# Turning the hidden rows of a 64-token expert slot: two row blocks stacked in one tile, four transposes a slot instead of eight

## The chip, the cores and the metric

The kernel runs on one core of a Trainium2 chip. The metric is the device time of one execution in microseconds (us), as a median of runs. The engines are TensorE (PE for its matmuls, PEld for its weight loads), VectorE (DVE), ScalarE (ACT), GpSimd (POOL) and SyncE (SP).

## The reference, cut

Attention over 24 heads feeds a dense two-layer block, and that feeds a mixture of eight experts in which each of the 896 tokens goes to one expert. The change lies in the last part:

```python
for e in range(E):                       # E = 8 experts, D = 768, F = 1024
    mask = expert_idx == e
    h = np.maximum(x[mask] @ w1[e], 0.0)
    out[mask] = gate_w[mask, None] * (h @ w2[e])
```

All inputs are float32. The kernel splits each operand into a high and a low part (`hi`, `lo`) and multiplies them in parts, so that one product of the reference is two or three matmul passes.

## The kernel before, in words

The expert part works on *slots*: a slot is up to so many tokens of one expert, which are gathered from `ydram`, multiplied by `w1` (`mm1`), passed through a ReLU, multiplied by `w2` (`mm2`), scaled by the gate and scattered to the output. An early slot and the remainder of the same expert (form M, 160 tokens) come first; then the slots run in the order T, M, T, L, T. Form L has up to 384 tokens, in two passes (D with 256, S with 128), form T has 64. So there are three T slots, called T1, T2 and T3 here; in the trace T1 lies at 413.4 to 427.4 us, T2 at 454.4 to 468.0, T3 at 520.2 to 532.8. Only they are changed; the S pass shares the function with them but keeps its own way.

In a T slot `mm1_x` takes the tokens as the stationary operand, high parts in columns 0 to 63, low parts in 64 to 127, and streams four blocks `q` of 256 weight columns. `two_pass` gives PSUM rows 0 to 63 (high) and 64 to 127 (low times high weights). For each `q` ScalarE copies the lower rows out (L1021) and VectorE adds the upper rows (L1022); the sum `hr` has 64 rows of tokens. Then the hidden units must be on partitions for `mm2`, so `turn` transposes `hr` on TensorE, two 128x128 transposes (L991) a block. Rows 64 to 127 of the tile are zeros that GpSimd wrote (L1015). ScalarE applies the ReLU for the high part (L994) and VectorE forms the low part (L995).

The order of the PE, ACT and DVE instructions in the slots is written out by hand: each engine runs them in program order. What is interleaved matters here:

- `turn(0)` and `turn(1)` stand before step `kc` 5 of `q` 2 and 3; `turn(2)` and `turn(3)` stand before steps `fc` 1 and 3 of `mm2` (`turn2=[1, 3]`).
- At the end of each `q`, behind the copy and the add, `pace` may put the split of one weight tile of the next slot into the queues: a 128x768 `mh` on ScalarE (L65) and an `ml` on VectorE (L72). The same is done after each `fc` of `mm2`. A T slot earns 0.5 of a split per `q` and 0.65 per `fc`.
- The evictions of the slot before (`osb`, L1069 to L1072) stand at the head of the ScalarE and VectorE queues when a T slot begins.
- The transposes of the next slot's tokens (`xt`, L1096) stand before `fc` 3 to 6 of `mm2`.

PSUM banks for `hps`, `ht` and `xt` come from `bank`, which goes round four of them.

Of the kernel before, what the change touches and what calls it, by code (L numbers as in the profile page):

```python
# [12 lines left out]
AF = mybir.ActivationFunctionType  # L13
ALU = mybir.AluOpType
# [6 lines left out]
P = 128  # L21
# [11 lines left out]
def f32(ap):  # L33
    return ap.bitcast(F32)


CFG = dict(
    first=1, hp=3000, xe=[1, 7, 8, 10, 12], turn=5, xfd=[3, 4, 5, 6], xfj=[1, 2, 3, 4],
    joint=1, mhi="A", rt6=[1, 4, 7, 9, 15], dve=(0, 1, 2, 3), neng=(),
    rs={2: [(1, 0), (2, 1)], 3: [(2, 2), (2, 0), (10, 1)], 4: [(1, 3), (5, 2)],  # L40
        5: [(2, 3), (2, 4), (3, 4), (4, 4), (5, 4), (7, 4)], 6: [(f, 5) for f in (1, 4, 7, 9, 15)]},
# [12 lines left out]
def build(tc, qkd, vd, w_in, w_out, emb, tau, wm, cst, out, dbg_y=None):  # L54
    nc = tc.nc
    V, A, G, T, DMA = nc.vector, nc.scalar, nc.gpsimd, nc.tensor, nc.sync
# [30 lines left out]
    ident = cpool.tile([P, P], F32, name="ident")  # L87
# [357 lines left out]
    for k in range(-3, 2 * NU + 2):  # L445
        u, h = divmod(k, 2)
# [376 lines left out]
    mo = {}  # L823
# [10 lines left out]
    def h_at(fs, part, n, m=1):  # L834

        hb = mo["h"][:, fs, part:part + m] if m > 1 else mo["h"][:, fs, part]
        return hb[..., 0:n], hb[..., n:2 * n]
# [3 lines left out]
    def bank(name):  # L841

        state["bank"] += 1
        if state["routed"] and state["bank"] % 4 == 0:
            return ps_r.tile([P, 512], F32, tag="lg", name=name)
        return ps_h.tile([P, 512], F32, tag="h", name=name)
# [47 lines left out]
    def pace(x, cap=2.7):  # L894

        if not fd["seq"]:
            return
        fd["credit"] = min(fd["credit"] + x, cap)
        while fd["credit"] >= 1 and fd["done"] < min(fd["free"], 16 * (len(fd["seq"]) - 1)):
            feed_one()  # L900
            fd["credit"] -= 1
# [22 lines left out]
    def mm1_w(s, w, hooks, fin=nop):  # L924
# [42 lines left out]
        fin(6)  # L967
        fin(7)

    def two_pass(os, x, whs, wls, k, n, m):  # L970

        def high():
            for o, w in zip(os, whs):
                T.matmul(o[0:2 * m], x, w, start=(k == 0), stop=(k == n - 1))  # L974

        if k == 0:
            high()
        for o, w in zip(os, wls):
            T.matmul(o[0:m], x[:, 0:m], w, start=False, stop=False)  # L979
        if k:  # L980
            high()

    def mm1_x(s, w, hooks, fin=nop):

        xh, xl = mo["xh"], mo["xl"]
        n = FORM[s[0]][0]

        def turn(q, hr):
            ht = bank("ht")[:, 0:2 * P].rearrange("p (a b) -> p a b", b=P)
            for j in range(2):  # L990
                T.transpose(ht[:, j], hr[:, j * P:(j + 1) * P], ident)  # L991
            ht = ht[:, :, 0:n]
            hi, lo = h_at(slice(2 * q, 2 * q + 2), 0, n)
            A.activation(hi, ht, AF.Relu)  # L994
            V.scalar_tensor_tensor(out=lo, in0=ht, scalar=0.0, in1=f32(hi), op0=ALU.max, op1=ALU.subtract)  # L995

        hrs = []
        for q in range(4):
            ps = bank("hps")[:, 0:256]
            for kc in range(KC):  # L1000
                step(hooks, (q, kc))
                if kc == CFG["turn"] and q >= 2:
                    turn(q - 2, hrs[q - 2])
                wh, wl = w[2 * q + kc // 3]
                c = slice((kc % 3) * 256, (kc % 3 + 1) * 256)
                if n == P:
                    T.matmul(ps, xh[:, kc, 0:P], wh[:, c], start=(kc == 0), stop=False)
                    T.matmul(ps, xh[:, kc, 0:P], wl[:, c], start=False, stop=False)
                    T.matmul(ps, xl[:, kc, 0:P], wh[:, c], start=False, stop=(kc == KC - 1))
                else:  # L1010
                    two_pass([ps], xh[:, kc, 0:P], [wh[:, c]], [wl[:, c]], kc, KC, n)
            if q % 2 == 0:
                hr2 = hpool.tile([P, 512], F32, tag="hs", bufs=4, name="hr")
                if n < P:
                    G.memset(hr2[n:P], 0.0)  # L1015
            hr_ = hr2[:, (q % 2) * 256:(q % 2 + 1) * 256]
            hr = hr_[0:n]
            if n == P:
                A.copy(hr, ps)
            else:  # L1020
                A.copy(hr, ps[64:P])  # L1021
                V.tensor_tensor(out=hr, in0=ps[0:64], in1=hr, op=ALU.add)  # L1022
            hrs.append(hr_)
            fin(2 * q)
            fin(2 * q + 1)
            pace(CFG["pc"][s[0]][0], CFG["cap"])

        rest = iter([lambda: turn(2, hrs[2]), lambda: turn(3, hrs[3])])
        return {t: [(f() for f in rest)] for t in CFG["turn2"]}

    def mm2(parts, w, hooks, split=False, fin=nop):

        at = (0, CFG["tail"] if split else 384, DM)
        col = [slice(at[c], at[c + 1]) for c in range(2)]
        pss = [[ps_y.tile([P, 512], F32, tag=f"y{c}", name="ops")[:, :at[c + 1] - at[c]] for c in range(2)]
               for _ in parts]
        for cs in ((0,), (1,)) if split else ((0, 1),):
            for fc in range(8):
                if cs[0] == 0:
                    step(hooks, fc)  # L1040
                wh, wl = w[8 + fc]
                for (s, part), ps in zip(parts, pss):
                    if FORM[s[0]][part] == P:
                        hh, hl = h_at(fc, part, P) if s[0] != "M" else (
                            mo["hm"][:, fc, 0:P], mo["hm"][:, fc, -P:])
                        for x, ww in ((hh, wh), (hh, wl), (hl, wh)):
                            for c in cs:
                                T.matmul(ps[c], x, ww[:, col[c]],  # L1048
                                         start=(fc == 0 and x is hh and ww is wh), stop=(fc == 7 and x is hl))
                    else:  # L1050
                        m = FORM[s[0]][part]
                        x = mo["hm"][:, fc, P:P + 2 * m] if s[0] == "M" else mo["h"][:, fc, part, 0:2 * m]
                        two_pass([ps[c] for c in cs], x,
                                 *([ww[:, col[c]] for c in cs] for ww in (wh, wl)), fc, 8, m)
                if cs[-1] == 1:
                    fin(8 + fc)
                    pace(CFG["pc"][parts[-1][0][0]][1])
        for (s, part), ps in zip(parts, pss):
            mm2_out(s, part, ps, col)

    def mm2_out(s, part, ps, cols):
        gi, si, gate = s[1][:3]
        col = s[2] + part
        n = FORM[s[0]][part]
        o = hpool.tile([P, DM], F32, tag="hs", bufs=4, name="osb")[0:n]
        for c in range(2):
            oc = o[:, cols[c]]
            if n == P:
                A.activation(oc, ps[c], AF.Copy, scale=gate[:, col:col + 1])  # L1069
            else:  # L1070
                A.activation(oc, ps[c][n:2 * n], AF.Copy, scale=s[1][3][n:2 * n, col:col + 1])
                V.scalar_tensor_tensor(out=oc, in0=ps[c][0:n], scalar=gate[0:n, col:col + 1], in1=oc,  # L1072
                                       op0=ALU.mult, op1=ALU.add)
        G.indirect_dma_start(out=out[:, :], out_offset=bass.IndirectOffsetOnAxis(ap=si[0:n, col:col + 1], axis=0),  # L1074
                             in_=o, in_offset=None, bounds_check=NT - 1, oob_is_err=False)
# [27 lines left out]
    def step(hooks, key):  # L1103
        for x in hooks.get(key, ()):
            next(x, None)
# [21 lines left out]
    def mm1(s, w, hooks, fin=nop):  # L1127
        return (mm1_w if s[0] in "DM" else mm1_x)(s, w, hooks, fin)
# [7 lines left out]
    for t in range(2, NTI):  # L1136
# [10 lines left out]
        if t == NTI - 1:  # L1147
# [6 lines left out]
            xe = slot_x(eslot)  # L1154
# [129 lines left out]
    def run_slot(ps, w, feeds, at_end=False):  # L1284

        def hooks_for(at, it, more=None):
            hooks = more or {}
            for k in at:
                hooks.setdefault(k, []).append(it)
            return hooks  # L1290

        s = ps[0]
        if len(ps) == 2:
            more = mm1(s, w, {})
            it = slot_x(ps[1])
            next(it)
            mm2([(s, 0)], w, hooks_for(CFG["xfd"], it, more))
            all_of(it)
            more = mm1(ps[1], w, {}, freed)
            it = feeds()  # L1300
            next(it, None)
            mm2([(s, 1), (ps[1], 0)], w, hooks_for(CFG["xfj"], it, more), fin=freed)
            all_of(it)
            return
        more = mm1(s, w, {}, freed)
        it = feeds()
        next(it, None)
        mm2([(s, i) for i in range(len(FORM[s[0]]))], w, hooks_for(CFG["xfd"], it, more), split=at_end, fin=freed)
        all_of(it)
# [140 lines left out]
```

## Time and profile before

| | |
|---|---|
| median of 3 runs | 542.87 us (542.78 to 543.02) |
| profiled execution | 543.2 us |
| its span, first to last instruction | 541.5 us |
| mean granted TensorE clock | 0.996 |
| PE busy | 527.2 us, 97% of the span |
| DVE, ACT, POOL busy | 413.5, 287.4, 205.6 us |

Times in the trace count from the start of the span. The profiled execution is 0.33 us above the median, and 1.7 us of it lie outside the span.

### The profile page before, as it was taken

The numbers are of one execution on the slowest core, as the hardware profiler recorded it, in microseconds if no ns is written. First come the engines' busy times: TensorE is split into PE (matmuls) and PEld (weight loads), VectorE is DVE, ScalarE is ACT, GpSimd is POOL, SyncE is SP. The second block draws the span as 40 slices with busy tenths as digits, with TensorE's granted clock in tenths as the row PEclk, the third lists the DMA queues.
The fourth block names the chain that finished last, engine by engine and source line by source line (L and its number), as shares of the span: only waits on it lengthen the run. The fifth ranks groups of instructions, "written<-read, shape, count | busy, mean of one in ns | idle before, by whom it ended". The sixth has DMA issues, their size and how long they took to land.

```text
span 541.5 us, 9616 instructions
## 1 busy us (share of the span) xinstructions
PE 527.2 (97%) x3374; PEld 496.2 (92%) x3374; DVE 413.5 (76%) x976; ACT 287.4 (53%) x635; POOL 205.6 (38%) x273
## 2 busy tenths in 40 slices
PE   7899999999999999999999999999999999999993
PEld 4799999889999999999999989999999999999992
DVE  7888899656887979597899776895296897983741
ACT  7889887315335242433332326631386887764651
POOL 7998899916635643231011201026201302400010
PEclk9999999999999999999999999999999999999998
DMA  5667674331546555358200019303978889984310
GB/s 183 177 156 170 146 230 111 117 117 58 176 131 217 167 183 176 120 174 274 79 30 30 16 31 408 159 2 110 346 231 274 266 281 364 272 279 154 119 53 7
DMA packets 28474, 89.22 MB, mean 165 GB/s; under 512 B 2926, under 2 KB 12270, under 8 KB 28416
## 3 DMA queue, kind: packets, MB, share of 16 engines
q1 hardware_dynamic: 26880, 82.23, 47.8%
q0 software_dynamic: 1536, 6.29, 3.1%
q8 instruction: 28, 0.46, 0.3%
q14 instruction: 30, 0.25, 0.1%
HBM read 78.39 MB, written 6.32 MB: 156 GB/s over the span
## 4 chain that ended last, share of the span: by engine, by line
PE 73%; DVE 14%; DMA 6%; issue 2%; ACT 2%; POOL 2%; SPq 0%; POOLq 0%; DVEq 0%; ACTq 0%
PE yps L639 16%; PE ops L1048 11%; PE pv L323 7%; PE s L261 5%; PE pt L305 4%; DVE w L128 4%; DVE w L130 3%; PE hps L942 3%; PE ops L974 3%; PE ops L979 3%; DMA raw<-in_w_in 2%; PE pa L347 2%; PE pa L348 2%; PE pa L349 2%; DVE w L126 2%
## 5 line engine op out<-in xcount | busy, mean ns | idle before, releaser
L72 DVE TENSOR_TENSOR ml<-xraw,mh 128x768 fp32r<-128x768 f32 x64 | 59.4, 954 | 9.8 <-ACT mh L65 9.3
L65 ACT ACTIVATE mh<-xraw 128x768 fp32r<-128x768 f32 x64 | 52.1, 843 | 7.2 <-PE ops L974 5.8
L1048 PE MATMUL ops<-mh,act 128*128 128x384 f32 x224 | 53.5, 341 | 0.0
L323 PE MATMUL pv<-pt,v 128*128 128x448 f32 (+7 forms) x288 | 47.1, 296 | 0.6 <-ACT pt L65 0.6
L287 POOL TENSOR_SCALAR p<-p,rs 128x192 f32<-128x192 f32 (+6 forms) x84 | 45.5, 564 | 2.6 <-DVE rs L283 2.3
L274 ACT ACTIVATE p<-s,mn 128x192 f32<-128x192 f32 (+6 forms) x84 | 39.8, 476 | 11.7 <-DVE mn L271 6.4
L261 PE MATMUL s<-kh,q 128*128 128x128 f32 (+6 forms) x168 | 44.0, 308 | 0.7 <-ACT p L274 0.7
L130 DVE SCALAR_TENSOR_TENSOR w<-raw,w 128x768 int32<-128x768 int32 x32 | 42.5, 1331 | 0.7
L323 PEld LDWEIGHTS pv<-pt,v 128*128 128x128 f32 (+1 forms) x288 | 38.5, 163 | 2.7 <-ACT pt L65 1.2
L1048 PEld LDWEIGHTS ops<-mh,act 128*128 128x128 f32 x224 | 39.2, 188 | 0.8
L1074 POOL DMA_INDIRECT out<-osb,fsi x10 | 10.1, 1015 | 77.7 <-ACT osb L1069 48.8
L72 DVE TENSOR_TENSOR ml<-mraw,mh 128x768 fp32r<-128x768 f32 x32 | 30.1, 956 | 11.3 <-ACT mh L65 10.9
L128 DVE SCALAR_TENSOR_TENSOR w<-raw,w 128x768 int32<-128x768 int32 x32 | 37.0, 1160 | 0.7
L736 POOL CAST gh<-g 128x1 fp32r<-128x1 f32 x7 | 3.5, 505 | 88.1 <-DVE OHs L730 32.3
L126 DVE TENSOR_SCALAR w<-raw 128x768 int32<-128x768 int32 x32 | 22.9, 715 | 17.4 <-POOL wi3l L72 7.3
L72 DVE TENSOR_TENSOR pt<-pt 128x512 fp32r<-128x512 f32 x48 | 32.4, 683 | 4.8 <-ACT pt L65 4.8
L353 ACT ACTIVATE relu<-pa 128x448 f32<-128x448 f32 x32 | 17.0, 539 | 34.7 <-PE pa L349 34.7
L271 DVE CUSTOM_DVE_ANT_0 s<-s,maskf 128x192 f32<-128x192 f32 (+6 forms) x77 | 32.0, 430 | 4.5 <-PE s L261 4.4
L65 ACT ACTIVATE hs<-h 128x512 fp32r<-128x512 f32 (+1 forms) x32 | 17.8, 573 | 29.6 <-PE yps L639 27.5
L261 PEld LDWEIGHTS s<-kh,q 128*128 128x128 f32 x168 | 30.6, 197 | 2.6 <-ACT p L274 1.5
L72 DVE TENSOR_TENSOR hs<-h,hs 128x512 fp32r<-128x512 f32 (+1 forms) x32 | 21.9, 689 | 12.4 <-ACT hs L65 12.1
L65 ACT ACTIVATE pt<-pt 128x512 fp32r<-128x512 f32 x48 | 28.2, 600 | 5.6 <-PE pt L305 5.6
(471 smaller groups left out, 1681.3 us busy)
## 6 DMA issues: line engine op xcount, KB each, us to landing
xraw<-in_wm SPq DMA_DIRECT2D x32, 768.0 KB, 6.0
raw<-in_w_in SPq DMA_DIRECT2D x16, 768.0 KB, 4.2
raw<-in_w_out SPq DMA_DIRECT2D x16, 768.0 KB, 4.2
mraw<-in_wm SPq DMA_DIRECT2D x16, 768.0 KB, 4.7
qk<-in_qkd SPq DMA_DIRECT2D x11, 448.0 KB, 4.7
q<-qs SPq DMA_DIRECT2D x20, 224.0 KB, 3.8
v<-in_vd SPq DMA_DIRECT2D x12, 256.0 KB, 3.3
eb<-edram SPq DMA_DIRECT2D x8, 384.0 KB, 6.0
```

The source lines that it names most:

```text
L65: return A.activation(out, in_, AF.Copy, scale=scale)
L72: return eng.tensor_tensor(out=lo, in0=x, in1=hi, op=ALU.subtract)
L126: V.tensor_scalar(out=w[:, x], in0=raw[:, x, 1], scalar1=3, scalar2=0x3FFFFFFF, op0=ALU.logical_shift_left, op1=ALU.bitwise_and)
L128: V.scalar_tensor_tensor(out=w[:, x], in0=raw[:, x, 1], scalar=-0x40000000, in1=w[:, x], op0=ALU.bitwise_and, op1=ALU.bitwise_or)
L130: V.scalar_tensor_tensor(out=w[:, x], in0=raw[:, x, 0], scalar=29, in1=w[:, x], op0=ALU.logical_shift_right, op1=ALU.bitwise_or)
L261: T.matmul(ss, d["q2"][:, c, :, :, x].rearrange("p a b -> p (a b)"), d[y][:, :n], start=i_ == 0, stop=i_ == 2 and not first)
L271: last["max"] = V.tensor_tensor_reduce(out=ss, in0=ss, in1=maskf[:, S - n:], scale=-1.0, scalar=3.0e38, op0=ALU.add, op1=ALU.min, accum_ou ...
L274: last["exp", units.index(u), c] = A.activation(d["p"][c][:, :n], ss, AF.Exp, bias=mn, scale=1.0 if first else -1.0, accum_out=d["sm"][:, ...
L287: last["norm"] = G.tensor_scalar(out=p, in0=p, scalar1=rs[:, COL[c]:COL[c] + 1], scalar2=1.0, op0=ALU.mult, op1=ALU.mult)
L323: T.matmul(d["pv"][:, j * P:S] if h else d["pv"][0:D, j * P:S], d[x][:, j, 1:3].rearrange("p a b -> p (a b)") if h else d[x][:, j, 0], pt[ ...
L639: T.matmul(ps[t][c][:, :384], x, w[:, c * 384:(c + 1) * 384], start=(f == 0 and w is wh and x is hi), stop=(f == NF - 1 and x is lo))
L1048: T.matmul(ps[c], x, ww[:, col[c]], start=(fc == 0 and x is hh and ww is wh), stop=(fc == 7 and x is hl))
```

## The change

For n < 128 the result of an even `q` goes to rows 0 to 63 of a tile and that of an odd `q` to rows 64 to 127 of the same columns. `turn_both` transposes the pair of blocks at once, with two full 128x128 transposes, and applies ReLU and low part to two column groups (`c` 0 and 1). The first call stands before `kc` 5 of `q` 2 (`turnb=(2, 5)`), the second before `fc` 2 of `mm2` (`turnc=2`). The memsets go. The hidden blocks lie in another order, which `turned` undoes when `mm2` reads them. Forms D, S, L and M run as before.

```diff
+    turn=5, turnb=(2, 5), turnc=2,
...
+    def turned(fc):
+        return fc // 4 * 4 + fc % 2 * 2 + fc % 4 // 2
...
+        def turn_both(q, hr):
+            ht = bank("ht")[:, 0:2 * P]
+            for j in range(2):
+                T.transpose(ht[:, j * P:(j + 1) * P], hr[:, j * P:(j + 1) * P], ident)
+            ht = ht.rearrange("p (a t) -> p a t", t=n)
+            for c in range(2):
+                hi, lo = h_at(slice(4 * q + c, 4 * q + 4, 2), 0, n)
+                A.activation(hi, ht[:, c::2], AF.Relu)
+                V.scalar_tensor_tensor(out=lo, in0=ht[:, c::2], scalar=0.0, in1=f32(hi), op0=ALU.max, op1=ALU.subtract)
...
-                if kc == CFG["turn"] and q >= 2:
+                if n == P and kc == CFG["turn"] and q >= 2:
                     turn(q - 2, hrs[q - 2])
+                elif n < P and (q, kc) == CFG["turnb"]:
+                    turn_both(0, hrs[0])
...
                 hr2 = hpool.tile([P, 512], F32, tag="hs", bufs=4, name="hr")
-                if n < P:
-                    G.memset(hr2[n:P], 0.0)
-            hr_ = hr2[:, (q % 2) * 256:(q % 2 + 1) * 256]
-            hr = hr_[0:n]
             if n == P:
+                hr = hr2[:, (q % 2) * 256:(q % 2 + 1) * 256]
                 A.copy(hr, ps)
             else:
-                A.copy(hr, ps[64:P])
-                V.tensor_tensor(out=hr, in0=ps[0:64], in1=hr, op=ALU.add)
-            hrs.append(hr_)
+                hr = hr2[:, 0:256]
+                own, other = (slice(0, 64), slice(64, P)) if q % 2 == 0 else (slice(64, P), slice(0, 64))
+                A.copy(hr[own], ps[other])
+                V.tensor_tensor(out=hr[own], in0=ps[own], in1=hr[own], op=ALU.add)
+            if n == P or q % 2:
+                hrs.append(hr)
...
+        if n < P:
+            return {CFG["turnc"]: [(turn_both(1, hrs[1]) for _ in range(1))]}
...
-                        x = mo["hm"][:, fc, P:P + 2 * m] if s[0] == "M" else mo["h"][:, fc, part, 0:2 * m]
+                        x = mo["hm"][:, fc, P:P + 2 * m] if s[0] == "M" else mo["h"][:, turned(fc), part, 0:2 * m]
```

## Rows read from the trace of the kernel before

**Rows 1.** The page, busy time and share of the span by engine.
```profile
PE 527.2 (97%) x3374; PEld 496.2 (92%) x3374; DVE 413.5 (76%) x976; ACT 287.4 (53%) x635; POOL 205.6 (38%) x273
```
**Rows 2.** Windows: length, busy PE, PEld, DVE, ACT, POOL, clock, DMA share, GB/s.
```profile
413.40:427.40 14.00, 13.95 (x104) 12.86 (x103) 11.67 (x22) 11.81 (x24) 4.47 (x4) 1.00 0.83 263
427.40:454.40 27.00, 27.00 (x183) 24.96 (x182) 25.58 (x49) 22.69 (x42) 4.38 (x5) 1.00 0.89 289
```
**Rows 3.** Chain of work that ended last, T2: start, length, piece.
```profile
461.38 0.22 PE ht L991 x2
461.60 0.35 PE ops L979 x2
```
**Rows 4.** Groups of instructions by line, 385 us to the end: busy, mean ns, idle.
```profile
L1015 POOL MEMSET hr<- 64x512 f32 x6 | 3.0, 530 | 13.7 <-PE ht L991 13.7
```
**Rows 5.** Timeline of T1, matmuls: start, length, instruction.
```profile
417.53 0.28 PE L974 MATMUL hps<-mh,act 128*128 128x256 f32 x1
417.85 0.41 PE L991 MATMUL ht<-ident,hr 128*128 128x128 f32 x2
...
419.96 0.51 PE L974 MATMUL ops<-mh,act 128*128 128x384 f32 x2
```
**Rows 6.** Timeline of T1, ScalarE.
```profile
416.70 0.37 ACT L1021 COPY hr<-hps 64x256 f32<-64x256 f32 x1
417.09 0.85 ACT L65 ACTIVATE mh<-mraw 128x768 fp32r<-128x768 f32 x1
417.84 0.35 ACT L1021 COPY hr<-hps 64x256 f32<-64x256 f32 x1
418.30 0.28 ACT L994 ACTIVATE act<-ht 128x128 fp32r<-128x128 f32 x1
418.60 0.37 ACT L1021 COPY hr<-hps 64x256 f32<-64x256 f32 x1
418.87 0.85 ACT L65 ACTIVATE mh<-mraw 128x768 fp32r<-128x768 f32 x1
```
**Rows 7.** Timeline of T1, VectorE.
```profile
416.24 1.13 DVE L1072 SCALAR_TENSOR_TENSOR osb<-ops,fgate,osb 32x384 f32<-32x384 f32 x2 [0.58 <-ACT osb L1071]
417.30 0.40 DVE L1022 TENSOR_TENSOR hr<-hps,hr 64x256 f32<-64x256 f32 x1
417.97 0.96 DVE L72 TENSOR_TENSOR ml<-mraw,mh 128x768 fp32r<-128x768 f32 x1 [0.27 <-ACT mh L65]
418.85 0.41 DVE L1022 TENSOR_TENSOR hr<-hps,hr 64x256 f32<-64x256 f32 x1
...
419.75 0.96 DVE L72 TENSOR_TENSOR ml<-mraw,mh 128x768 fp32r<-128x768 f32 x1
```
**Rows 8.** Timeline of T2, VectorE's second add, and matmuls.
```profile
458.18 0.41 DVE L1022 TENSOR_TENSOR hr<-hps,hr 64x256 f32<-64x256 f32 x1
...
458.43 0.38 PE L991 MATMUL ht<-ident,hr 128*128 128x128 f32 x2
...
460.51 0.51 PE L974 MATMUL ops<-mh,act 128*128 128x384 f32 x2
```
**Rows 9.** Timeline of T3, all engines.
```profile
523.69 0.42 DVE L1022 TENSOR_TENSOR hr<-hps,hr 64x256 f32<-64x256 f32 x1 [0.93 <-ACT hr L1021]
...
524.27 0.38 PE L991 MATMUL ht<-ident,hr 128*128 128x128 f32 x2
...
527.78 0.96 DVE L72 TENSOR_TENSOR ml<-mraw,mh 128x768 fp32r<-128x768 f32 x1 [0.33 <-ACT mh L65]
...
528.99 0.19 PEld L974 LDWEIGHTS ops<-mh,act 128*128 128x128 f32 x1 [0.43 <-DVE act L995]
...
532.50 0.28 PE L974 MATMUL ops<-mh,act 128*128 128x256 f32 x1
```
**Rows 10.** Windows behind the last matmul, columns as in Rows 2.
```profile
535.00:537.00 2.00, 0.00 (x0) 0.00 (x0) 0.00 (x0) 0.00 (x0) 0.00 (x0) 1.00 0.07 14
537.00:539.00 2.00, 0.00 (x0) 0.00 (x0) 0.00 (x0) 0.00 (x0) 0.00 (x0) 0.58 0.03 8
```

More of the change, by code (lines that the diff above doesn't have):

```diff
@@ L37 @@
 CFG = dict(
-    first=1, hp=3000, xe=[1, 7, 8, 10, 12], turn=5, xfd=[3, 4, 5, 6], xfj=[1, 2, 3, 4],
+    first=1, hp=3000, xe=[1, 7, 8, 10, 12], turn=5, turnb=(2, 5), turnc=2, xfd=[3, 4, 5, 6], xfj=[1, 2, 3, 4],
     joint=1, mhi="A", rt6=[1, 4, 7, 9, 15], dve=(0, 1, 2, 3), neng=(),
```

## The prediction

> **What bounds the kernel now.** I read the page first, then windows of the expert slots, then the chain of work that ended last, and at the end the timelines of the three T slots, engine by engine. The page shows TensorE with work in 97% of the span [rows 1]. That is an average, so I looked at the stage of the change: in T1 PE is busy 13.95 of 14.00 us at the full clock, and in the M slot behind it 27.00 of 27.00 [rows 2]. The chain of work goes through the matmuls of the T slots, transposes included [rows 3]. So in this stretch what TensorE does not do comes off the end, and each time it waits is added to the end; there is no slack behind a T slot that would take a wait up. The other engines matter only through what they hand over late. All times here are of the one profiled execution, 543.2 us (span 541.5); I give the forecast against the median, 542.87, since only the difference is worked out.
>
> **What is removed.** First, transposes. A pair takes 0.22 us of TensorE's order, and the next piece starts right behind it [rows 3]. Four pairs a slot become two; three slots give 6 pairs x 0.22 = 1.32 us. The bounds: a pair hidden behind a wait gives nothing; one on the path gives 0.22. The same row carries the price of what stays, since the new transposes have the shape of the old ones; the zero rows were streamed as full tiles. A page prices this lower: the Trainium skill (TensorE: Matmul & The Clock Gate, section "Back-to-back issue gap") has about 81 ns for a 128-column matmul in a stream of loads and matmuls, so 12 of them would give an estimated 0.97 us and the forecast would be 0.35 us later. I go by the row.
>
> Second, the six memsets: 530 ns each on GpSimd [rows 4]. GpSimd waited 13.7 us before two of them and nobody is named as waiting for them, so I take nothing. If one of them did hold a scatter up, that scatter leaves earlier; only the very last scatter sets the end, and no memset lies in the last 20 us. Both bounds are 0.
>
> **What is the same.** Copies, adds, ReLUs and low parts keep their number and shapes: two of 128x2x64 elements for a pair of blocks, as before. The copy of an odd block now crosses to other partitions, but so did every copy before (rows 64 to 127 to rows 0 to 63). `mm2` reads the blocks in another order at no cost. Each slot takes two PSUM banks less, in a ring of four: what is reused is always four calls back and long read. I cost these at 0.
>
> **What moves, first call.** Before, the transposes in front of step 5 of `q` 2 needed block 0 only. Now they need block 1 as well, one block later, and block 1 gets through ScalarE and VectorE behind other work. All matmuls behind the transposes stand in TensorE's program order, so all of them wait.
>
> T1: the last matmul before the transposes started at 417.53, the transposes began at 417.85, because block 0's add ended at 417.70 (417.30 + 0.40) [rows 5, 7]; that gives 0.15 us from the end of an add to the transposes. That add was late since VectorE was busy until 417.37 with the evictions of the slot before. Block 1 is later by more than a block: ScalarE runs a weight split at 417.09 before the copy at 417.84 [rows 6], and VectorE runs the other half of the split, 0.96 us, from 417.97 to 418.93, before the add of block 1, which ends at 418.85 + 0.41 = 419.26 [rows 7]. Nothing in this string waits for TensorE, so it keeps its times after the change. New start of the transposes: 419.26 + 0.15 = 419.41, against 417.85: +1.56 us.
>
> T2: here VectorE is ahead, but again a split stands before the add of block 1, which ends at 458.18 + 0.41 = 458.59; transposes at 458.74 against 458.43 [rows 8]: +0.31.
>
> T3: the add ends at 523.69 + 0.42 = 524.11, transposes possible at 524.26, and TensorE comes at 524.27 [rows 9]: 0.
>
> Then the second pair inside `mm1` is gone: -0.22 in each slot.
>
> **What moves, second call.** It stands before `fc` 2 of `mm2` and needs block 3. In T1 I follow the string from the first call's transposes, with the distances of before: ReLU 0.45 later (417.85 to 418.30), the second ReLU 0.30 behind, the copy of block 2 0.30 behind that, the split 0.27 behind, its VectorE half 0.88 behind (418.87 to 419.75) and 0.96 long [rows 6, 7], then the add of block 3, which before began 0.08 ahead of the split's recorded end, 0.41 long, and 0.15 to the transposes: 0.45 + 0.30 + 0.30 + 0.27 + 0.88 + 0.96 - 0.08 + 0.41 + 0.15 = 3.64 us. TensorE needs from the same point to its `fc` 2: up to `mm2` 419.96 - 417.85 = 2.11, less the pair that is gone 0.22 [rows 5], plus two `fc` of 2 x 0.35 each [rows 3]: 3.29. It waits 0.35. In T2 the way to `mm2` is 460.51 - 458.43 = 2.08 [rows 8], so the wait is 0.38. Bounds: 0 if the split is later in the queue, 0.5 if the latency is counted to the weight loads.
>
> Behind it the hidden blocks 4 and 6 are needed at `fc` 4; in T1 and T2 TensorE has two `fc` and two groups of token transposes until then, and I see no further wait. The pair before `fc` 3 is gone: -0.22 in T1 and T2.
>
> In T3 there is a wait already: at 528.99 TensorE had stood 0.43 us for a low part that VectorE made behind a split (527.78 + 0.96) [rows 9]. The split follows the copy of block 3, and that comes one pair, 0.22, sooner. So what happens in front of this wait is swallowed by it, and the slot gains between 0 and 0.22; I take 0.15.
>
> **Sum.** T1: 1.56 - 0.22 + 0.35 - 0.22 = +1.47. T2: 0.31 - 0.22 + 0.38 - 0.22 = +0.25. T3: -0.15. Together +1.57, so 542.87 + 1.57 = 544.4 us, 0.29% slower. The work taken away is real, but three quarters of the sum of waits is one wait in T1. About 0.2% (1.09 us) is what a measurement of this kernel can tell from no change.
>
> **Rivals.**
>
> *The transposes come off and nothing waits* (the other side). Mechanism: the split that `pace` puts between the adds of blocks 0 and 1 does not hold the add up in the new order. For it: TensorE is the bound, and in T3 the add is in time. Against it: in T1 the add must end by 417.70 where it ended at 419.26; without the split (0.96) it would still end at about 418.3. It decides only if 1.56 us vanish from that string. It gives 542.87 - 1.32 = 541.5.
>
> *Only the first call waits.* The second string is worked out, not read; if block 3 comes in time, 0.35 and 0.38 fall away: 543.7, and if T2's first wait goes too, 543.4. For it: its distances are from other pairs of instructions. Against it: the split stands there in each of the two slots.
>
> *The delay spreads.* In the M slot behind T1 VectorE is busy 25.58 of 27.00 us [rows 2], 1.42 to spare, and T1's waits are 1.56 + 0.35 = 1.91. If VectorE idled as long and had to make it up there, TensorE would wait 0.49 more: 544.9. Against it: TensorE comes to that slot later by nearly the same time.
>
> *The clock falls.* After the last matmul, which ends at 532.78, the granted clock is still 1.00 in the window to 537 and is 0.58 in the next [rows 9, 10]; the wait of some 1.6 us in T1 is well under that. If it fell to the lower level (1.2 instead of 2.4 GHz) for the rest of T1, the 9.4 us from 418.0 on would double: 553.8. The Trainium skill (the same page, section "What's actually happening") holds that the throttled state is the default and activity releases it, which is what speaks for this rival; only the fall at the end shows it here.
>
> **How the numbers follow.** Forecast 0.62, only the first call waits 0.18, the delay spreads 0.11, nothing waits 0.08, the clock falls 0.01. The forecast's own bounds are +1.0 (first wait of T2 and half the second ones gone) to +2.1 (second waits 0.5 each, T3 at 0, page's price for the transposes), so a little of it lies under the 1.09 us. Slower than 0.2%: 0.70; within: 0.21; faster: 0.09. The range goes from 543.4 (only the first call waits, T1 alone) to 545.2 (forecast, second waits 0.5 each, and part of the spread).
>
> **What would show it.** In the profile after: the transposes line with 20 instead of 32 matmuls and no memset line; in T1 an idle of TensorE of 1.6 to 1.8 us before the first transposes with VectorE's add of block 1 ending just ahead; about 0.3 in T2, none in T3; an idle of 0.3 to 0.4 before the second transposes in T1 and T2; T1 longer by about 1.5, M and L as long as before. The prediction is wrong if the add of block 1 in T1 ends before 418.5, if the split no longer stands before it, or if the M slot behind T1 becomes shorter by what T1 lost.

## The result, and the profile after

The changed kernel takes 546.52 us as the median of five runs (545.48 to 547.62), against 543.01 us (542.78 to 543.45): a ratio of 1.0059, 95% interval 1.0047 to 1.0071. It is slower by 0.6%, where 0.29% was forecast and 545.2 us was the upper end of the range.

The page of the changed kernel, busy time by engine:

```profile
PE 528.7 (97%) x3361; PEld 496.8 (91%) x3362; DVE 414.6 (76%) x976; ACT 287.7 (53%) x635; POOL 201.8 (37%) x267
```

It says next to nothing, since it hardly differs from [rows 1]. Windows, cut at the first matmul of a slot, say more. Their columns are the length, then the busy time of PE, PEld, DVE, ACT and POOL, the granted clock, the DMA share and GB/s; the lines are T1, the M slot, T2, and T3 with its evictions.

```profile
414.26:429.88 15.62, 13.44 (x97) 12.09 (x97) 11.45 (x21) 11.79 (x23) 5.08 (x4) 1.00 0.61 195
429.88:457.00 27.12, 27.12 (x183) 25.09 (x183) 26.07 (x50) 22.72 (x42) 2.54 (x2) 1.00 0.91 313
457.00:471.20 14.20, 13.46 (x97) 12.35 (x97) 10.23 (x19) 10.66 (x22) 4.64 (x4) 1.00 0.80 285
523.72:536.40 12.68, 12.29 (x85) 10.32 (x84) 5.51 (x11) 6.04 (x14) 1.99 (x2) 1.00 0.15 58
```

TensorE now has an idle of 2.2 us in T1, where [rows 2] showed next to none, and of 0.7 us in T2; the M slot is full as before. For all comparisons below the slots are measured in one way: from the start of a slot's first matmul to that of the next, T3 to the start of its last matmul, from the matmul timelines. Before, they are T1 13.66, M 27.12, T2 13.46, L 52.43, T3 12.21 us; after, 15.62, 27.12, 14.20, 52.52, 12.37. The sum is 2.95 us longer. The spans differ by 3.3: T1 also begins 0.64 us later in this execution, which has to do with the kernel's first microseconds (last section), and the tail behind the last matmul is 0.3 shorter.

T1 after the change, matmuls:

```profile
418.17 0.28 PE L978 MATMUL hps<-mh,act 128*128 128x256 f32 x1
420.09 0.44 PE L1004 MATMUL ht<-ident,hr 128*128 128x128 f32 x2 [1.64 <-DVE hr L1037]
...
422.02 0.52 PE L978 MATMUL ops<-mh,act 128*128 128x384 f32 x2
...
424.12 0.44 PE L1004 MATMUL ht<-ident,hr 128*128 128x128 f32 x2 [0.54 <-DVE hr L1037]
```

Here are the two waits. In brackets stands the idle time before an instruction and what ended it: both times VectorE's add, of block 1 and of block 3. VectorE in the same stretch:

```profile
417.94 0.40 DVE L1037 TENSOR_TENSOR hr<-hps,hr 64x256 f32<-64x256 f32 x1
418.61 0.96 DVE L72 TENSOR_TENSOR ml<-mraw,mh 128x768 fp32r<-128x768 f32 x1 [0.27 <-ACT mh L65]
419.60 0.43 DVE L1037 TENSOR_TENSOR hr<-hps,hr 64x256 f32<-64x256 f32 x1
420.87 0.29 DVE L1009 SCALAR_TENSOR_TENSOR act<-ht,act 128x128 fp32r<-128x128 f32 x1 [0.84 <-ACT act L1008]
421.51 0.29 DVE L1009 SCALAR_TENSOR_TENSOR act<-ht,act 128x128 fp32r<-128x128 f32 x1 [0.34 <-ACT act L1008]
421.90 0.42 DVE L1037 TENSOR_TENSOR hr<-hps,hr 64x256 f32<-64x256 f32 x1
422.65 0.96 DVE L72 TENSOR_TENSOR ml<-mraw,mh 128x768 fp32r<-128x768 f32 x1 [0.33 <-ACT mh L65]
423.64 0.43 DVE L1037 TENSOR_TENSOR hr<-hps,hr 64x256 f32<-64x256 f32 x1
```

The string of [rows 7] is there: add, split, add, and TensorE goes on 0.06 us behind the second add. Below it stands what was not forecast. ScalarE:

```profile
418.61 0.36 ACT L1036 COPY hr<-hps 64x256 f32<-64x256 f32 x1
420.56 0.28 ACT L1008 ACTIVATE act<-ht 128x128 fp32r<-128x128 f32 x1 [1.59 <-PE ht L1004]
421.20 0.28 ACT L1008 ACTIVATE act<-ht 128x128 fp32r<-128x128 f32 x1 [0.36 <-DVE act L1009]
421.50 0.37 ACT L1036 COPY hr<-hps 64x256 f32<-64x256 f32 x1
421.77 0.84 ACT L65 ACTIVATE mh<-mraw 128x768 fp32r<-128x768 f32 x1
422.64 0.37 ACT L1036 COPY hr<-hps 64x256 f32<-64x256 f32 x1
```

The second ReLU comes 0.64 us after the first, not 0.30 as the forecast had it, and the bracket says why: it waited for VectorE's first low part. What stands behind it in ScalarE's order (the copy of block 2, a split, the copy of block 3) is put off by the 0.34 us. T2 and T3, matmuls:

```profile
461.37 0.44 PE L1004 MATMUL ht<-ident,hr 128*128 128x128 f32 x2 [0.19 <-DVE hr L1037]
...
465.41 0.44 PE L1004 MATMUL ht<-ident,hr 128*128 128x128 f32 x2 [0.55 <-DVE hr L1037]
```
```profile
527.70 0.38 PE L1004 MATMUL ht<-ident,hr 128*128 128x128 f32 x2
...
530.94 0.44 PE L1004 MATMUL ht<-ident,hr 128*128 128x128 f32 x2 [0.29 <-DVE hr L1037]
```

The first call waits in T2 and not in T3, as [rows 8, 9] had let expect; the second call waits in all three.

### The profile page after: what moved, and what is told of

The parts are those of the page before. It is cut to its first block, busy times and chain, and to the rows that moved or that the text cites. A ratio compares the mean times of both kernels' runs of the same rounds, so it can differ in the third digit from the quotient of the medians.

```text
span 544.8 us, 9582 instructions
## 1 busy us (share of the span) xinstructions
PE 528.7 (97%) x3361; PEld 496.8 (91%) x3362; DVE 414.6 (76%) x976; ACT 287.7 (53%) x635; POOL 201.8 (37%) x267
## 4 chain that ended last, share of the span: by engine, by line
PE 84%; DVE 8%; ACT 3%; issue 2%; DMA 1%; POOL 1%; SPq 0%; POOLq 0%; DVEq 0%; ACTq 0%
PE yps L639 14%; PE ops L1066 11%; PE pa L347 7%; PE pa L348 7%; PE pa L349 7%; PE pv L323 7%; PE s L261 6%; PE pt L305 4%; PE hps L942 3%; PE ops L978 2%; DVE ml L72 2%; PE ops L983 2%; PE hps L960 2%; PE hps L961 2%; PE hps L962 2%
## 5 line engine op out<-in xcount | busy, mean ns | idle before, releaser
L261 PE MATMUL s<-kh,q 128*128 128x128 f32 (+6 forms) x168 | 45.4, 318 | 0.4 <-ACT p L274 0.4
L261 PEld LDWEIGHTS s<-kh,q 128*128 128x128 f32 x168 | 31.8, 205 | 2.2 <-ACT p L274 1.1
```

The source lines that it names most:

```text
L261: T.matmul(ss, d["q2"][:, c, :, :, x].rearrange("p a b -> p (a b)"), d[y][:, :n], start=i_ == 0, stop=i_ == 2 and not first)
```

## The experiments

Two theories stood at the start. A: the loss is made in the T slots, by adds that stand behind weight splits and by the second ReLU that waits for the first low part. B: half of it is made elsewhere (a late start of that execution, or VectorE as the next limit). What A and B mean in the expectation of each run is said there. All slot lengths in us; the ratio is against the kernel before on the same chip, with its 95% interval.

| kernel | T1 | M | T2 | L | T3 | sum against before | ratio |
|---|---|---|---|---|---|---|---|
| before | 13.66 | 27.12 | 13.46 | 52.43 | 12.21 | | |
| changed | 15.62 | 27.12 | 14.20 | 52.52 | 12.37 | +2.95 | 1.0059 (1.0047 to 1.0071) |
| changed, again | 15.60 | 27.13 | 14.17 | 52.58 | 12.36 | +2.96 | 1.0051 (1.0038 to 1.0064) |
| one ReLU a pair | 15.08 | 27.12 | 13.66 | 52.42 | 12.28 | +1.68 | 1.0026 (1.0017 to 1.0035) |
| splits behind blocks 1, 3 | 14.23 | 27.22 | 13.03 | 53.53 | 12.39 | +1.52 | 1.0029 (1.0018 to 1.0039) |
| eight transposes, moved | 14.95 | 27.11 | 13.56 | 52.42 | 12.11 | +1.27 | 1.0022 (1.0013 to 1.0030) |
| two ReLUs, outputs apart | 15.62 | 27.12 | 14.20 | 52.51 | 12.54 | +3.11 | 1.0053 (1.0039 to 1.0067) |
| one ReLU, splits behind 1, 3 | 13.62 | 27.12 | 13.00 | 52.44 | 12.28 | -0.42 | 0.9994 (0.9983 to 1.0005) |
| one ReLU, first split behind 1 | 13.84 | 27.13 | 13.26 | 52.46 | 12.28 | +0.09 | 1.0003 (0.9993 to 1.0013) |
| memsets back | 15.60 | 27.13 | 14.24 | 52.57 | 12.38 | +3.04 | one run, 546.76 us |
| two PSUM banks | 15.02 | 27.13 | 13.63 | 52.45 | 12.13 | +1.48 | 1.0022 (1.0013 to 1.0031) |
| ReLU, ReLU, low, low | 15.16 | 27.12 | 13.72 | 52.43 | 12.15 | +1.70 | 1.0031 (1.0018 to 1.0043) |
| one ReLU, splits late | 13.62 | 27.12 | 16.68 | 55.41 | 11.83 | +5.78 | 1.0105 (1.0089 to 1.0121) |
| one ReLU, 1 and 3, T3 late | 13.62 | 27.13 | 13.00 | 52.44 | 11.83 | -0.86 | 0.9981 (0.9969 to 0.9992) |

**The changed kernel again.** No edit.

> The changed kernel once more. Theory A (waits in the T slots: block 1's add behind a weight split, block 3's add behind another, and, new, the second ReLU of a pair behind the first low part): 2.9 us above before, the same three slots longer by 2.0, 0.7 and 0.2 us. Theory B (half of the loss is a late start in that one execution: its matmuls were 1.0 us late at 15 us and 0.6 us late at the start of T1): a trace without the late start, and a median nearer to +2.3 us.

The slots repeat within 0.06 us: +2.96. T1 starts late here too (414.23). So the slots are the steady part of the loss: 2.95 us, where the forecast had 1.57, and the other 1.4 us are to be explained. Theory B's late start is real, but the slots lose as much without counting it, and it is no part of the change: the run below that keeps the eight transposes has it too (T1 from 414.25).

**One ReLU a pair.** The four blocks lie in the same places, so one instruction can take them.

```diff
-            for c in range(2):
-                hi, lo = h_at(slice(4 * q + c, 4 * q + 4, 2), 0, n)
-                A.activation(hi, ht[:, c::2], AF.Relu)
-                V.scalar_tensor_tensor(out=lo, in0=ht[:, c::2], ...)
+            hi, lo = h_at(slice(4 * q, 4 * q + 4), 0, n)
+            A.activation(hi, ht, AF.Relu)
+            V.scalar_tensor_tensor(out=lo, in0=ht, ...)
```

> One ReLU and one low part over all four blocks of a pair instead of two of each over every second block; nothing else changed. Theory A: the copies of blocks 2 and 3 are no longer behind ReLU, low part, ReLU, so the second wait falls from 0.70 to about 0.2 us in T1 and T2 and the waits of T3 (0.29 and 0.23) nearly go: 1.3 us faster than the changed kernel, still 1.6 us slower than before; the first waits (1.64 and 0.3) stay. Theory B: no change against the changed kernel beyond 0.4 us.

1.27 us less than the changed kernel, as A has it. In T1 and T2 all of it comes from the second product (7.32 and 7.35 us instead of 7.86 and 7.90); the first wait stays: T1's first product takes 7.76 us in both. Only T3 gains little, 0.09, where its waits of 0.29 and 0.23 were expected to nearly go: a wait of 0.26 us goes over to the low part, which now does both halves behind a split.

**Splits behind blocks 1 and 3.**

```diff
-            pace(CFG["pc"][s[0]][0], CFG["cap"])
+            if n == P:
+                pace(CFG["pc"][s[0]][0], CFG["cap"])
+            elif q % 2:
+                pace(2 * CFG["pc"][s[0]][0], CFG["cap"])
```

> In the T slots the weight splits of the first product are put into the queues behind blocks 1 and 3 only, as many as before, so that none stands between the adds of a pair. Theory A: the first wait falls from 1.64 to about 0.6 us in T1 (the evictions of the slot before still hold it) and to 0 in T2, the second wait to 0 in both: 2.5 to 2.9 us faster than the changed kernel, level with before within 0.5 us. Theory B: the waits only move to the weights, or the loss lies elsewhere: less than 1 us faster.

Matmuls of this kernel in T1 and at the start of the L slot, and VectorE ahead of each:

```profile
418.05 0.44 PE L1004 MATMUL ht<-ident,hr 128*128 128x128 f32 x2 [0.42 <-DVE hr L1037]
...
468.92 0.39 PE L961 MATMUL hps<-act,mh 128*128 128x256 f32 x1 [0.70 <-DVE act L72]
```
```profile
416.08 1.13 DVE L1093 SCALAR_TENSOR_TENSOR osb<-ops,fgate,osb 32x384 f32<-32x384 f32 x2 [0.58 <-ACT osb L1092]
417.14 0.86 DVE L1037 TENSOR_TENSOR hr<-hps,hr 64x256 f32<-64x256 f32 x2
...
467.45 0.95 DVE L72 TENSOR_TENSOR ml<-xraw,mh 128x768 fp32r<-128x768 f32 x1
468.32 1.02 DVE L72 TENSOR_TENSOR act<-xt,act 128x384 fp32r<-128x384 f32 x2
```

The first wait falls from 1.64 to 0.42 us in T1, and the first product by 1.23; in T2 it goes (5.89 instead of 6.30). So the split between the adds is what held them. The 0.42 that is left stands behind the evictions of the slot before: the two adds follow them at once. But the L slot becomes 1.1 us longer: its second matmul waits for the low part of its tokens (`act<-xt`), which stands behind a split on VectorE. With one ReLU a pair besides (below) the L slot loses nothing, so the serial ReLUs have a part in this. Both theories are right about a part: 1.43 instead of 2.5 to 2.9 us.

**Eight transposes, moved.** The kernel before with the calls at the places of the changed one.

```diff
-                if kc == CFG["turn"] and q >= 2:
+                if n == P and kc == CFG["turn"] and q >= 2:
                     turn(q - 2, hrs[q - 2])
+                elif n < P and (q, kc) == (2, 5):
+                    turn(0, hrs[0])
+                    turn(1, hrs[1])
...
+        if n < P:
+            r2 = list(rest)
+            return {2: [([f() for f in r2] for _ in range(1))]}
```

> The kernel before with its eight transposes, memsets and tiles, but called at the places of the changed kernel: those of blocks 0 and 1 before step 5 of block 2, those of blocks 2 and 3 before step 2 of the second product. Only the lateness, none of the gain. Theory A: T1 longer than before by 1.6 + 0.4, T2 by 0.3 + 0.4, T3 by 0.1: 2.7 us slower than before, since the six pairs of transposes stay and the low parts of two pairs don't overlap. Theory B: slower by 1.6 at most.

A miss: +1.27 us, not 2.7. Matmuls in T1, and VectorE's add of block 3:

```profile
418.48 0.41 PE L991 MATMUL ht<-ident,hr 128*128 128x128 f32 x2
419.94 0.44 PE L991 MATMUL ht<-ident,hr 128*128 128x128 f32 x2 [1.05 <-DVE hr L1025]
...
423.27 0.60 PE L991 MATMUL ht<-ident,hr 128*128 128x128 f32 x4
```
```profile
422.74 0.41 DVE L1025 TENSOR_TENSOR hr<-hps,hr 64x256 f32<-64x256 f32 x1
```

Block 0's pair and its ReLU run while block 1's add is awaited. So only one ReLU is left ahead of the copy of block 2, block 3's add ends at 423.15, before TensorE comes to the second call, and the second wait is gone altogether (second products 7.32 and 7.35 us, as before). This tells where the gain of the change went. With the lateness of the new places but all eight transposes, the slots lose 1.27 us; with four transposes and the ReLUs unchained (two PSUM banks, below) they lose 1.48. Once the calls stand where they must wait, taking transposes out saves nothing: block 0's pair would have run in the first wait, and for most of the time that block 2's pair takes (0.22 us) TensorE waits in the other run (0.11 us in T1 and 0.14 in T2, from the start of the second product, less the 1.41 us of its first two steps).

**Two ReLUs, outputs apart.**

```diff
-            for c in range(2):
-                hi, lo = h_at(slice(4 * q + c, 4 * q + 4, 2), 0, n)
-                A.activation(hi, ht[:, c::2], AF.Relu)
-                V.scalar_tensor_tensor(out=lo, in0=ht[:, c::2], ...)
+            for c in (0, 2):
+                hi, lo = h_at(slice(4 * q + c, 4 * q + c + 2), 0, n)
+                A.activation(hi, ht[:, c:c + 2], AF.Relu)
+                V.scalar_tensor_tensor(out=lo, in0=ht[:, c:c + 2], ...)
```

> The changed kernel with two ReLUs and two low parts a pair as it has them, but the first takes blocks 0 and 1 of the four and the second blocks 2 and 3, so that what they write no longer interleaves. Theory A (the second ReLU waits for the first low part because their outputs interleave in one tile): the second ReLU starts 0.30 us behind the first, as before the change, the second wait of T1 and T2 falls from 0.70 to about 0.35, T1 about 15.3, T2 about 13.9, T3 about 12.2 us: 0.9 us faster than the changed kernel. Theory B (two instructions a pair are too many, however they lie; merging them helped by their number): second ReLU still 0.64 behind the first, no gain.

No gain: T1 and T2 as in the changed kernel. ScalarE in T1:

```profile
421.99 0.28 ACT L1008 ACTIVATE act<-ht 128x128 fp32r<-128x128 f32 x1 [1.59 <-PE ht L1004]
422.63 0.28 ACT L1008 ACTIVATE act<-ht 128x128 fp32r<-128x128 f32 x1 [0.36 <-DVE act L1009]
```

Still 0.64. The reason I had formed, outputs that interleave, falls.

**Two PSUM banks.** What else the two ReLUs and low parts share is the PSUM tile that they read.

```diff
-            ht = bank("ht")[:, 0:2 * P]
             for j in range(2):
-                T.transpose(ht[:, j * P:(j + 1) * P], hr[:, j * P:(j + 1) * P], ident)
-            ht = ht.rearrange("p (a t) -> p a t", t=n)
-            for c in range(2):
-                hi, lo = h_at(slice(4 * q + c, 4 * q + 4, 2), 0, n)
-                A.activation(hi, ht[:, c::2], AF.Relu)
-                V.scalar_tensor_tensor(out=lo, in0=ht[:, c::2], ...)
+                ht = bank("ht")[:, 0:P]
+                T.transpose(ht, hr[:, j * P:(j + 1) * P], ident)
+                ht = ht.rearrange("p (a t) -> p a t", t=n)
+                hi, lo = h_at(slice(4 * q + 2 * j, 4 * q + 2 * j + 2), 0, n)
+                A.activation(hi, ht, AF.Relu)
+                V.scalar_tensor_tensor(out=lo, in0=ht, ...)
```

> The changed kernel, but each of the two transposes of a pair has a PSUM bank of its own, with one ReLU and one low part on each. Theory A (the second ReLU waits since both ReLUs and both low parts read one PSUM tile in turn, ScalarE, VectorE, ScalarE): in the first call the second ReLU starts 0.30 us behind the first instead of 0.64, the second wait of T1 and T2 falls from 0.70 to about 0.35: T1 15.3, T2 13.9 us, 0.7 us faster than the changed kernel in the slots. Theory B (it is what they write, not what they read): 0.64 as before, no gain.

ScalarE in T1, both ReLUs in one row of the view (`x2`):

```profile
420.88 0.45 ACT L1007 ACTIVATE act<-ht 128x128 fp32r<-128x128 f32 x2 [1.48 <-PE ht L1004]
421.35 0.37 ACT L1035 COPY hr<-hps 64x256 f32<-64x256 f32 x1
```

The pair takes 0.45 us with no wait inside, the copy of block 2 starts 0.47 behind the first ReLU instead of 0.94, and the slots lose 1.48 us instead of 2.95, twice the gain that was expected. With the outputs the same as in the run before, it is the shared PSUM tile that chains the two engines: while ScalarE and VectorE read one tile in turn, the program puts a wait between every change of reader. Here a tile is also a bank, so the runs don't tell which of the two it goes by.

**ReLU, ReLU, low, low.**

```diff
-            for c in range(2):
-                hi, lo = h_at(slice(4 * q + c, 4 * q + 4, 2), 0, n)
-                A.activation(hi, ht[:, c::2], AF.Relu)
-                V.scalar_tensor_tensor(out=lo, in0=ht[:, c::2], ...)
+            hl = [h_at(slice(4 * q + c, 4 * q + 4, 2), 0, n) for c in range(2)]
+            for c in range(2):
+                A.activation(hl[c][0], ht[:, c::2], AF.Relu)
+            for c in range(2):
+                V.scalar_tensor_tensor(out=hl[c][1], in0=ht[:, c::2], ...)
```

> The changed kernel with the four instructions of a pair in another order: both ReLUs, then both low parts; one PSUM bank, outputs as in the changed kernel. Theory A: ScalarE reads the bank twice in a row, so the second ReLU follows at 0.30 and the copies of blocks 2 and 3 come 0.34 sooner: T1 15.3, T2 13.9 us. Theory B (it is what they write): the same, since no low part stands between them; so this run can't tell A from B, but tells both from a third: that the two ReLUs are slow by themselves (then 0.64 stays).

+1.70 us, T1 15.16 and T2 13.72: with the reader changing once instead of three times, one bank does nearly as well as two. The ReLUs are not slow by themselves.

**One ReLU and splits behind blocks 1 and 3** is both edits above together.

> Both edits together: one ReLU and one low part a pair, and splits behind blocks 1 and 3 only. Theory A: T1 about 13.8 (the evictions of the slot before still hold the first add, a wait of 0.4), T2 about 13.0, T3 about 12.3 us; the L slot behind T2 loses less than the 1.1 us it lost with the second edit alone, since VectorE is done sooner with the pair, say 0.5: level with before within 0.4 us. Theory B (VectorE is the next limit: what the slots gain, the next slot waits for its tokens' low parts): L slot still longer by 1 us or more, 0.5 us slower than before.

As A has it, and better: T1 13.62, T2 13.00, and the L slot loses nothing (52.44). The sum is 0.42 us under before; the interval of the ratio still holds 1.

**One ReLU, only the first split moved.** Besides the one ReLU a pair:

```diff
-            pace(CFG["pc"][s[0]][0], CFG["cap"])
+            if n == P or q > 1:
+                pace(CFG["pc"][s[0]][0], CFG["cap"])
+            elif q:
+                pace(2 * CFG["pc"][s[0]][0], 1.5)
```

> One ReLU and one low part a pair, and only the split behind block 0 is put behind block 1; the other splits stay where they are. Theory A: first wait of T1 0.4 instead of 1.64, of T2 0; second waits 0 to 0.2: T1 about 13.9, T2 about 13.3, T3 12.3, M and L as before: level with before within 0.3 us. Theory B: the L or M slot behind gets longer by what was gained.

Level with before, as expected: T1 13.84, T2 13.26.

**Memsets back**, `G.memset(hr2[n:P, 256:512], 0.0)` for each tile of a T slot; they are half as wide as the old ones.

> The changed kernel with six memsets of 64x256 elements put back into the unused half of its tiles. If the memsets cost nothing, every slot as long as in the changed kernel (T1 15.6, T2 14.2, T3 12.4 us) within 0.1. If GpSimd's order counted, the slots behind them differ.

Every slot is within 0.06 us of the changed kernel: these memsets cost nothing.

**One ReLU, splits late.** Besides the one ReLU a pair:

```diff
-            pace(CFG["pc"][s[0]][0], CFG["cap"])
+            if n == P:
+                pace(CFG["pc"][s[0]][0], CFG["cap"])
+            elif q == 1:
+                pace(2 * CFG["pc"][s[0]][0], CFG["cap"])
...
-                    pace(CFG["pc"][parts[-1][0][0]][1])
+                    k = parts[-1][0][0]
+                    pace(CFG["pc"][k][1] if k != "T" else 0.87 if fc > 1 else 0.0)
```

> One ReLU and one low part a pair; in the T slots one split behind block 1, none behind block 3, and those of the second product only from step 2 on, behind the second pair. Theory A: T1 about 13.6, T2 about 13.0 as with splits behind blocks 1 and 3, and T3 11.9 instead of 12.28, since no split stands before its second low part: 0.8 us faster than before in the slots, if the M and L slots keep 27.1 and 52.4. Theory B (VectorE is the next limit): the splits that come later make the M slot, where VectorE is busy 25.6 of 27 us, or the start of L longer by as much.

T1 and T3 come out as theory A has them (13.62, 11.83), but T2 and L lose 6.2 us. TensorE's weight loads in the expert part and what they waited for (total, times, longest):

```profile
PEld ops L983 <- DVE ml L72: 4.1, 5, 1.6
PEld hps L962 <- DVE ml L72: 1.4, 2, 0.7
```

Both wait for the low parts of weight tiles (`ml`). So the splits can't be put off that far: most of the wait, 3.8 us, lies in T2's second product, whose weights are late. Theory B is right about the start of L and wrong about the M slot, which keeps its 27.12 us; T2 was in neither theory.

**One ReLU, splits behind 1 and 3, in T3 behind 1 only.** The edit is shown against the run with one ReLU and splits behind 1 and 3.

```diff
-            elif q % 2:
+            elif q == 1 or q == 3 and fd["now"] < NSS:
                 pace(2 * CFG["pc"][s[0]][0], CFG["cap"])
```

> One ReLU and one low part a pair, splits behind blocks 1 and 3 only, and in T3 none behind block 3, so that the last tile's split falls behind the second pair by itself. Theory A: T1 13.6, T2 13.0, T3 11.8, M 27.1 and L 52.4 us as in the runs that had each: 0.9 us less than before in the slots, some 0.16% faster. Theory B (the last split, made late, holds the matmuls that read it): T3 12.3 or more, level with before.

Faster than before, and the only one whose interval lies below 1: a median of 542.25 us (541.93 to 544.36, 12 runs) against 543.59 (542.60 to 544.65, 17 runs), ratio 0.9981 (0.9969 to 0.9992), 0.86 us less in the slots. Its calls in T1 and T3:

```profile
418.39 0.44 PE L1004 MATMUL ht<-ident,hr 128*128 128x128 f32 x2 [0.42 <-DVE hr L1036]
421.71 0.38 PE L1004 MATMUL ht<-ident,hr 128*128 128x128 f32 x2
...
523.96 0.38 PE L1004 MATMUL ht<-ident,hr 128*128 128x128 f32 x2
526.91 0.44 PE L1004 MATMUL ht<-ident,hr 128*128 128x128 f32 x2
```

What is left of the waits at the calls is the 0.42 us of T1, behind the evictions of the slot before. T2, which has none, takes 13.00 us against 13.46: 0.46 less, or two pairs at 0.22 us each.

## Why the prediction was wrong in size

**Right, and shown.** TensorE is the bound of this stretch and nothing behind a T slot takes a wait up: the M slot is 27.12 us in both. The transposes fall from 32 to 20 matmuls (12 and 8 on their two lines) and the memsets, put back, cost nothing. The first call waits for the add of block 1 behind a weight split. Its three terms were +1.56, +0.31 and 0; counted from the start of each slot the first transposes come later by 1.60 (420.09 - 414.26 against 417.85 - 413.62), 0.34 and 0.00 us. That T1 fits to 0.04 us is in part luck: the add of block 1 ended 0.13 us later in the slot than before (5.77 us after its start against 5.64), and the transposes followed it by 0.06 us where 0.15 was taken. Putting the split behind block 1 takes 1.2 us of the 1.60 away.

**The step that failed** is in "What is the same": the ReLUs and low parts "keep their number and shapes", costed at 0, and from it the distance in the string of the second call, "the second ReLU 0.30 behind". Number and shapes were indeed the same. What changed is that both ReLUs and both low parts of a call now read one PSUM tile, so that the second ReLU waits for the first low part; in T1 and T2 it came 0.64 us behind. The second call's wait was forecast at 0.35 and 0.38 us in T1 and T2; counted from the start of the second product with 1.41 us for two steps (two of two groups of 0.35 each), it was 424.12 - 422.02 - 1.41 = 0.69 and 465.41 - 463.30 - 1.41 = 0.70. The forecast with 0.64 in place of 0.30 would have been 0.69 and 0.72. In T3 the first call's low part itself stood behind a split on VectorE, and the second ReLU came 1.18 us behind the first:

```profile
528.12 0.28 ACT L1008 ACTIVATE act<-ht 128x128 fp32r<-128x128 f32 x1 [0.16 <-PE ht L1004]
529.30 0.28 ACT L1008 ACTIVATE act<-ht 128x128 fp32r<-128x128 f32 x1 [0.91 <-DVE act L1009]
```

There the second call, whose wait was to be swallowed, waited 0.29 at the transposes, and the slot became 0.16 longer, not 0.15 shorter. Against the forecast that is 0.34, 0.32 and 0.31 us, 1.0 of the 1.4 us that the slots lost beyond it; the rest, some 0.15 in T1 and in T2 and 0.09 in L, is not traced to one term. With two PSUM banks the second ReLU comes 0.17 us behind the first, less than the 0.30 of the forecast, and the slots give +1.36, +0.17 and -0.08. The forecast with 0.17 in place of 0.30 is +1.34, +0.12 and -0.15. So the rest of the sum holds, and reading one tile in turn cost 1.5 us against two banks.

The rows of the T slots before could not have shown it: there each block's two transposes had a bank of their own, which one ReLU and one low part read, in [rows 6, 7] too. The Trainium skill (PSUM — Partial Sum Buffer, section "PSUM bank collisions raise a hardware error") has a rule that bears on it: reads of one bank by ScalarE and VectorE at the same time collide, as any other two accesses of two engines do, and the compiler's back end puts a dependency between such instructions. The changed kernel's row agrees: 0.36 us of wait on VectorE's read.

Two figures of the prediction don't add up, without bearing on this. The one wait in T1 is 60% of the sum of waits (1.56 of 2.60), not three quarters. And the terms named for its bounds give +0.9 and +2.3, not +1.0 and +2.1.

**The rivals.** "Only the first call waits" and "nothing waits" fall with the rows. "The delay spreads" falls: M has the same length. "The clock falls" is out: the granted clock is 1.00 in T1 with its wait of 1.64 us. The removed transposes were costed at 0.22 us a pair on the path; the run with eight transposes at the new places shows that this holds only where nothing waits, and T2 of the last run, which has no wait, that it holds there.

## What to carry to other kernels

Work taken from the bounding engine is a gain only where that engine would have been ready; if the same edit makes it wait for a later operand, the removed instructions are the ones that would have filled the wait. So look first at what stands ahead of the new operand in the in-order queues that make it, and move that. And give two engines that read results in turn one tile each, or one instruction each: whoever changes reader pays a handover.

## What the runs showed that was not expected

A handover between ScalarE and VectorE on one PSUM tile costs as much as what stands ahead of the reader, and TensorE more than itself. It put ScalarE 0.34 us behind the forecast in T1 and T2 and 0.88 in T3, where a split stood ahead of the low part; that is 1.5 us in the slots against two banks, because copies and splits stood behind it.

The kernel's first 12 us differ between executions. The three 512-column matmuls of the warm-up in the changed kernel, and the same three in the kernel before:

```profile
8.33 1.47 PE L392 MATMUL wp<-wz 128*128 128x512 bf16 x3
```
```profile
7.37 0.81 PE L392 MATMUL wp<-wz 128*128 128x512 bf16 x3
```

They took 1.47 us in seven of the fourteen profiled executions and 0.81 in the other seven, though the granted clock reads 1.00 in both. T1 began between 413.2 and 415.7 us, and not by this alone: the run with the memsets, with 0.81, began it at 414.42. The kernel before, run more often beside the experiments, spread over 542.53 to 544.66 us where its first five runs lay within 0.7. The slot lengths repeat within 0.1 us all the same, which is why the experiments are read by them. What sets the pace of the start was not tried.
